# Batch 0's first pass in an attention and MoE kernel: casts shared out differently, the last sums on the matrix engine, weights loaded once

## The chip, the core and the metric

The kernel runs on one core of one Trainium2 chip. The metric is the device time of one execution in microseconds (us). A core has five engines that run side by side, each taking its own instructions in order: TensorE (PE: matmuls, PEld for its weight loads), VectorE (DVE), ScalarE (ACT), GpSimd (POOL) and SyncE (SP, which here only starts transfers). Transfers between the chip's memory and the core's SBUF are done by 16 DMA engines; a transfer is started by an instruction on POOL or SP.

## The reference

```python
def _attn_ref(x, inducing):          # x: 4 x 12480 x 128, inducing: 32 x 128
    scale = 1.0 / np.sqrt(C)
    I = np.broadcast_to(inducing[None], (B, m, C))
    def mab(q, kv):
        s = scale * (q @ kv.transpose(0, 2, 1))
        s = s - s.max(-1, keepdims=True)
        a = np.exp(s)
        a /= a.sum(-1, keepdims=True) + 1e-09
        return a @ kv
    h = mab(I, x)                    # 32 rows of each batch from all its rows
    return mab(x, h)

def _moe_ref(x, w_in, w_out):        # w_in: 128 x 2048, w_out: 2048 x 128
    h = x @ w_in
    relu6 = np.clip(h + 3.0, 0.0, 6.0)
    g = h * relu6 / 6.0
    return g @ w_out
```

The output is the second function applied to the rows of the first, 49920 x 128 in float32.

## The kernel before, in words

Each of the four batches goes through three phases.

**Phase A** reads the batch's 12480 rows once, in seven groups (`groups`, numbered 0 to 6): six of 128 partitions x 16 rows (1 MB each) and one of 96 x 2 rows. For each group the rows are cast to bf16 (`a_cast`, in quarters 0 to 4 of the 16 rows), transposed on PE into PSUM and copied out by DVE (`a_T`, two halves, L290 and L291), multiplied by the inducing rows (`a_s1`, L298), exponentiated on ACT (L304), and summed with those weights on PE (`a_agg`, L314, into the PSUM tile `hnd`). The denominators are summed by DVE over all groups in `dacc` (L325, L327).

**Phase C** reduces `dacc` (`c_sum`, L419), forms the 32 denominators on PE and divides (`c_den`, L432 to L438), transposes the result H (`c_HT`), and derives from it a small matrix product with the MoE weights: sixteen blocks `c_sq` (matmul L583, squared on ACT L594 or DVE L591 and L592) and `c_C` (L603), and `c_G3` (L489), `c_hs`, `c_L`, `c_BD` (L573, L577) for a linear part. `w_low` (L916, POOL) makes the low halves of w_in that `c_G3` reads.

**Phase B** passes over the batch's rows again, in 25 chunks, mainly on PE (L827, L856, L875) with ACT, DVE and POOL beside it, and writes the output. It needs `Cq` (`c_tail`) and `BD`.

Batch 0's phases A and C stand alone at the start (`a_first`, `c_first`); the order of every instruction on every engine there is written out by hand. From then on the kernel's main loop runs phase B of a batch, with the phases A and C of the next batch spliced in by position (`a_units`, `c_units`, `bg`). The order on each engine is the order of the program, so an instruction that waits holds up all that follow it on its engine.

`warm(n)` issues n matmuls of 512 columns with no use for their result. The rows of x come in five buffers (`XBUF`): the load of group 5 waits for group 0's buffer. Loads start on POOL's queue, in program order with POOL's casts. In `a_first` the cast of group g+1 is issued ahead of the transposes of group g:

```python
for g in range(NGR):
    if g + 1 < NGR:
        cast(g + 1)          # 3/4 on ACT, 1/4 on POOL (groups 1 to 3) or DVE
    a_T(0, g, 0)
    ...
    a_T(0, g, 1)
    ...
    if late:
        a_agg(0, g - 1, 0, late)
        a_agg(0, g - 1, 1, late)
    a_s1(0, g)
```

`load_weights` brings w_in and w_out twice each: once cast to bf16 by the transfer (`w_in_b`, `w_out_b`), once in float32 (`w_in_r`, two halves, and `w_out_r`).

Of the kernel before, what the change touches and what calls it, by code (L numbers as in the profile page):

```python
# [24 lines left out]
TG = 16  # L25
# [5 lines left out]
CASTLEAD = 1.6  # L31

# [18 lines left out]
def kernel(  # L51
# [40 lines left out]
    with ExitStack() as es:  # L92
# [71 lines left out]
        def load_weights(i):  # L164
            w_out = moe_w_out.rearrange("(kb kp) c -> kp kb c", kp=P)
            if i == 0:
                nc.gpsimd.dma_start(w_in_b[:, :], moe_w_in[:, :])
            elif i == 1:
                nc.gpsimd.dma_start(w_out_b[:, :, :], w_out)
                for h in range(2):  # L170
                    t = dgp.tile([P, F // 2], FP32R, name="w_in_r", tag="dg")
                    nc.gpsimd.dma_start(t[:, :], moe_w_in[:, h * F // 2 : (h + 1) * F // 2])
                    w_in_r.append(t)
                nc.gpsimd.dma_start(w_out_r[:, :, :], w_out)
# [25 lines left out]
        eng.memset(ones[:, :], 1.0)  # L200
        blk_f = const.tile([P, P], FP32, name="blk_f")
# [17 lines left out]
        for i in range(2):  # L219
            t = const.tile([P, 512], FP32R, name=f"BD{i}")  # L220
            eng.memset(t[:, :].bitcast(FP32), 0.0)
            BD.append(t)
# [70 lines left out]
        def a_s1(b, g):  # L293
            t0, p, n = groups[g]
            st = S[b]
            s1 = side_bank(b, [P, 512], FP32, "s1")
            for i in range(n):
                nc.tensor.matmul(  # L298
                    s1[:p, i * M : (i + 1) * M],
                    lhsT=st[("xT", g)][:, i * p : (i + 1) * p],  # L300
                    rhs=I_T[:, :],
                )
            a1 = a1p.tile([P, TG * M], FP32R, name="a1")
            nc.scalar.activation(a1[:p, : n * M], s1[:p, : n * M], ACT.Exp, scale=scale)  # L304
            st["a1"] = a1

        def a_agg(b, g, h, a1):
            t0, p, n = groups[g]
            st = S[b]
            lo, hi = (0, n // 2) if h == 0 else (n // 2, n)  # L310
            if g == 0 and h == 0:
                st["hnd"] = psH.tile([P, 512], FP32, name="hnd", tag="hnd")
            for i in range(lo, hi):
                nc.tensor.matmul(  # L314
                    st["hnd"][:M, :C],
                    lhsT=a1[:p, i * M : (i + 1) * M],
                    rhs=xs[(b, g)][:p, i, :],
                    start=(g == 0 and i == 0),
                    stop=(g == NGR - 1 and i == n - 1),
                )  # L320
            if h == 0:
                if b == 0 and g == NGR - 1:
                    pass
                elif g == 0:
                    nc.vector.tensor_copy(st["dacc"][:p, : n * M], a1[:p, : n * M].bitcast(FP32))  # L325
                else:
                    nc.vector.tensor_add(  # L327
                        st["dacc"][:p, : n * M], st["dacc"][:p, : n * M], a1[:p, : n * M].bitcast(FP32)
                    )
            else:  # L330
                if b == 0 and g == NGR - XBUF:
                    load_weights(1)
                load_next(b, g)
                if b == 0 and g == NGR - XBUF - 1:
                    load_weights(0)
# [48 lines left out]
        def a_first():  # L384

            def cast(g):
                eng = nc.gpsimd if 1 <= g <= 3 else nc.vector
                a_cast(0, g, ((nc.scalar.copy, 0, 2), (nc.scalar.copy, 2, 3), (eng.tensor_copy, 3, 4)))

            a_cast(0, 0, ((nc.scalar.copy, 0, 2), (nc.scalar.copy, 2, 4)))  # L390
            late = None
            for g in range(NGR):
                if g + 1 < NGR:
                    cast(g + 1)
# [4 lines left out]
                if g == 0:  # L399
                    warm(4)  # L400
                if late:
                    a_agg(0, g - 1, 0, late)
                    a_agg(0, g - 1, 1, late)
                a_s1(0, g)
                if g == 0:
                    warm(4)
                late = S[0]["a1"]
            half_rows()
            a_agg(0, NGR - 1, 0, late)
            a_agg(0, NGR - 1, 1, late)  # L410


        def c_sum(b, main=True):

            st = S[b]
            dred = cst.tile([P, M], FP32, name="dred" if main else "dred1")
            src = st["dacc"] if main else st["a1"].bitcast(FP32)
            p, n = (P, TG) if main else groups[-1][1:]
            nc.vector.tensor_reduce(  # L419
                dred[:p, :],  # L420
                src[:p, : n * M].rearrange("p (s m) -> p m s", m=M),
# [3 lines left out]
            st["dred"] = st.get("dred", []) + [dred[:p, :]]  # L425

        def c_den(b):
            st = S[b]
            dps = psF.tile([P, 512], FP32, name="dps", tag="fb")
            dred = st.pop("dred")  # L430
            for k, d in enumerate(dred):
                nc.tensor.matmul(  # L432
                    dps[:M, :2], lhsT=d, rhs=ones[: d.shape[0], :], start=(k == 0), stop=(k == len(dred) - 1)
                )
# [116 lines left out]
        def c_L(b, h):  # L551
# [15 lines left out]
            nc.vector.tensor_scalar_mul(L[:, :], lp[:M, :C], -1.0 / 6.0)  # L567
            st["L"] = L

        def c_BD(b):  # L570
# [4 lines left out]
            for q in range(4):  # L575
                eng = nc.vector.tensor_copy if q % 2 else nc.scalar.copy
                eng(bd[32 * q : 32 * q + 32, q * C : (q + 1) * C], lt[32 * q : 32 * q + 32, :C])  # L577
# [79 lines left out]
        def c_first():  # L657

            c_sum(0)
            c_sum(0, False)  # L660
            warm(2)
# [13 lines left out]
            for i in range(F // 256):  # L675
                w_low(i)
            bg(-3.5)
            load_held(3, len(held))
            for jb in range(3, 6):
                sq(jb)  # L680
                cs(jb - 3)
            b_f(0, 0)
            b_base(0, 0, 0)
            b_base(0, 0, 1)
            sq(6)
            cs(3)
# [226 lines left out]
        def w_low(i):  # L913
            lo, hi = i * 256, (i + 1) * 256
            t, at = w_in_r[2 * lo // F], lo % (F // 2)
            nc.gpsimd.tensor_sub(w_in_l[:, lo:hi], t[:, at : at + 256].bitcast(FP32), w_in_b[:, lo:hi])  # L916
# [257 lines left out]
```

## Time and profile before

| | us |
|---|---|
| median of 3 runs (310.03 to 311.34) | 310.95 |
| the profiled execution's own time | 310.18 |
| its span, first to last instruction | 308.3 |
| outside the span | 1.88 |
| group 1, 2, 3, 4, 5 of x at hand (ACT's cast starts) | 9.64, 12.19, 14.68, 18.44, 21.10 |
| transposes of groups 3, 4, 5 start on PE | 15.78, 20.33, 23.89 |
| the division of batch 0 (L436) starts | 29.78 |
| main loop's first matmul (L856) | 47.17 |
| last matmul of the main loop ends, about | 302.5 |

All times after the fourth line are counted from the span's start, in the profiled execution. PE is busy 94% of the span, DVE 76%, ACT 73%, POOL 38%. In the lines of the timeline that the prediction shows, the columns are: start, duration, engine, line of the kernel, operation, what it writes <- what it reads with the shapes, the number of instructions merged, and in square brackets the engine's idle time ahead of them with what ended it. The end of a PE row includes the time until the result can be read; the spacing of rows, not their duration, is what an engine needs for one.

### The profile page before, as it was taken

How to read it: one execution, taken by the hardware profiler on the slowest of the kernel's cores; microseconds unless marked ns; L12 is line 12 of the kernel's file. 1: busy time of each engine (PE TensorE's matmuls, PEld its weight loads, DVE VectorE, ACT ScalarE, POOL GpSimd, SP SyncE). 2: the span in 40 equal slices, each digit the busy share in tenths (PEclk: the TensorE clock that was granted, in tenths of full speed). 3: DMA queues.
4: the chain of work that ended last, by engine and by line, in shares of the span. 5: the costliest groups of instructions: out<-in, count | busy, mean ns of one | idle time of the engine just before them, and what ended most of it. 6: DMA issues, size and time to landing. Idle time of an engine off the chain costs nothing. (4 is left out here: it accounts for less than half of the span.)

```text
span 308.3 us, 9788 instructions
## 1 busy us (share of the span) xinstructions
PE 288.8 (94%) x3942; PEld 230.3 (75%) x3963; DVE 234.3 (76%) x499; ACT 224.9 (73%) x431; POOL 117.4 (38%) x234
## 2 busy tenths in 40 slices
PE   8978989999999899999998999998898999999992
PEld 3876577989888678777887977786687777777881
DVE  1567757887998578678897859788877885988893
ACT  3662769776968989668798899665696787777760
POOL 8460852431019995010097745000577760000000
PEclk9989999999999999999999999999999999999997
DMA  6999779699965547979628425256445565576753
GB/s 218 423 288 323 199 253 373 210 378 307 361 204 163 194 151 228 393 225 291 223 57 308 164 64 179 95 159 198 157 135 139 179 197 184 177 235 216 214 205 120
DMA packets 27441, 67.73 MB, mean 220 GB/s; under 512 B 5216, under 2 KB 20352, under 8 KB 21504
## 3 DMA queue, kind: packets, MB, share of 16 engines
q1 hardware_dynamic: 18784, 38.36, 38.4%
q0 software_dynamic: 8608, 28.71, 31.0%
q8 instruction: 32, 0.52, 0.7%
q14 instruction: 17, 0.14, 0.1%
HBM read 29.77 MB, written 25.56 MB: 179 GB/s over the span
## 5 line engine op out<-in xcount | busy, mean ns | idle before, releaser
L834 ACT ACTIVATE TF<-bp 128x512 bf16<-128x512 f32 (+1 forms) x200 | 115.6, 589 | 33.4 <-PE bp L827 17.9
L875 PE MATMUL op<-Cq,TF 128*128 128x128 bf16 (+1 forms) x784 | 104.7, 221 | 0.3
L875 PE MATMUL op<-Cq,TD 128*128 128x128 bf16 (+1 forms) x784 | 102.5, 219 | 0.0
L892 DVE TENSOR_TENSOR os<-op,r_all 128x512 f32<-128x512 f32 (+1 forms) x100 | 67.4, 674 | 23.5 <-PE op L875 18.9
L845 DVE TENSOR_TENSOR TD<-TF,d 128x1024 bf16<-128x1024 bf16 (+1 forms) x100 | 75.6, 756 | 4.3 <-ACT TF L834 3.3
L875 PEld LDWEIGHTS <-TF 128*128 128x128 bf16 (+1 forms) x784 | 55.1, 98 | 24.1 <-issue 12.7
L827 PE MATMUL bp<-xT,W 128*128 128x512 bf16 (+1 forms) x184 | 68.6, 375 | 2.2 <-DVE nf_all L753 1.0
L875 PEld LDWEIGHTS <-TD 128*128 128x128 bf16 (+1 forms) x784 | 60.3, 98 | 0.7 <-issue 0.2
L856 PE MATMUL op<-BD,nf 128*128 128x512 f32 (+1 forms) x100 | 52.3, 523 | 0.2 <-DVE os L892 0.2
L279 ACT CAST xb<-xr 128x512 bf16<-128x512 f32 (+1 forms) x70 | 45.3, 661 | 8.2 <-DMA xr<-in_x_dram 8.1
L291 DVE COPY xT<-pt 128x1024 bf16<-128x1024 bf16 (+1 forms) x56 | 34.0, 616 | 16.7 <-PE pt L290 15.8
L519 POOL TENSOR_TENSOR dg<-G 128x256 f32<-128x256 f32 x48 | 40.1, 836 | 0.0
L518 POOL TENSOR_TENSOR dg<-G 128x256 f32<-128x256 f32 x48 | 31.3, 653 | 14.6 <-ACT sq L526 10.1
L516 POOL COPY gate<-TD 128x1 bf16<-128x1 bf16 x48 | 11.7, 244 | 62.3 <-DVE TD L845 61.6
L526 ACT ACTIVATE sq<-dg 128x512 bf16<-128x512 f32 x48 | 30.3, 633 | 2.9 <-POOL dg L519 2.9
L314 PE MATMUL hnd<-xr,a 128*32 128x128 f32 x384 | 31.8, 229 | 0.6 <-ACT a L304 0.6
L290 PE MATMUL pt<-ident_b,xb 128*128 128x128 bf16 x392 | 30.9, 222 | 0.0
L603 PE MATMUL cp<-w_out_b,sq 128*128 128x128 bf16 x256 | 24.7, 219 | 2.5 <-ACT TF L834 1.3
L314 PEld LDWEIGHTS hnd<-xr,a 128*32 128x32 f32 x384 | 25.5, 111 | 1.7 <-ACT a L304 0.7
L783 PE MATMUL rp<-one,nf 128*128 128x4 f32 (+1 forms) x100 | 26.2, 264 | 0.5 <-ACT TF L834 0.5
L290 PEld LDWEIGHTS <-xb 128*128 128x128 bf16 x392 | 24.1, 99 | 2.8 <-issue 1.3
L806 ACT ACTIVATE dk<-pp 128x512 bf16<-128x512 f32 (+1 forms) x28 | 15.6, 556 | 12.3 <-PE pp L799 11.3
(127 smaller groups left out, 384.5 us busy)
## 6 DMA issues: line engine op xcount, KB each, us to landing
xr<-in_x_dram POOLq DMA_DIRECT2D x23, 1024.0 KB, 7.7
out_dram<-os SPq DMA_DIRECT2D x23, 1024.0 KB, 4.1
d<-dk SPq DMA_DIRECT2D x96, 128.0 KB, 4.4
xr<-in_x_dram POOLq DMA_DIRECT2D x2, 512.0 KB, 4.7
w_in_r<-in_moe_w_in_dram POOLq DMA_DIRECT2D x2, 512.0 KB, 10.7
w_out_r<-in_moe_w_out_dram POOLq DMA_DIRECT2D x1, 1024.0 KB, 14.1
out_dram<-os SPq DMA_DIRECT2D x4, 256.0 KB, 3.5
w_in_b<-in_moe_w_in_dram POOLq DMA_DIRECT2D x1, 512.0 KB, 7.7
```

What stands on the lines that cost most here:

```text
L279: eng(xb[:p, lo:hi, :], xs[(b, g)][:p, lo:hi, :].bitcast(FP32))
L290: nc.tensor.transpose(pt[:, (i - lo) * p : (i - lo + 1) * p], xb[:p, i, :], ident_b[:p, :p])
L291: nc.vector.tensor_copy(st[("xT", g)][:, lo * p : hi * p], pt[:, : (hi - lo) * p])
L314: nc.tensor.matmul(st["hnd"][:M, :C], lhsT=a1[:p, i * M : (i + 1) * M], rhs=xs[(b, g)][:p, i, :], start=(g == 0 and i == 0), stop=(g == NG ...
L518: nc.gpsimd.tensor_sub(dg[:, 0], stepped(G2, jb, 0, 1, 0), stepped(G2, jb, 2, 0, 2))
L519: nc.gpsimd.tensor_sub(dg[:, 1], stepped(G2, jb, 1, -1, 0), stepped(G2, jb, 10, 0, 2))
L827: nc.tensor.matmul(bp[:, :w], lhsT=st["W"][:, k].rearrange("p m i -> p (m i)"), rhs=st[("xT", g)][:, j * w : (j + 1) * w],)
L834: nc.scalar.activation(st[("x", c)][:, k, :w], bp[:, :w], ACT.Exp, scale=scale)
L845: nc.vector.tensor_mul(u[:, :, :w], t[:, :, :w], d[:, :w].unsqueeze(1).to_broadcast([P, 2, w]))
L856: nc.tensor.matmul(op[:p, : S_ * C], lhsT=st[("nf", g)][:R, j * p : (j + 1) * p], rhs=st["BD"][:R, : S_ * C], start=True, stop=False, skip ...
L875: nc.tensor.matmul(op[:p, s * C : (s + 1) * C], lhsT=T[k][:, s * p : (s + 1) * p], rhs=st["Cq"][:, k, :], start=False, stop=(s == S_ - 1 a ...
L892: nc.vector.tensor_mul(ot[:p, j * S_ : (j + 1) * S_, :], op[:p, : S_ * C].rearrange("p (s c) -> p s c", c=C), r_all[:p, b, c, :S_].unsquee ...
```

## The change

In `a_first`, the cast of group g is now issued in its own iteration: half on ACT, a quarter on DVE and a quarter on POOL (groups 1 to 3), or half on DVE (groups 4 and 5); group 6 is cast by POOL. The exponentials of a group follow the next group's cast on ACT. Two `warm` matmuls follow the scores of groups 0 to 4. `half_rows` moves to iteration 2. The scores and exponentials of group 5 are done in two halves, and the PE sums of group 5 come after the scores of group 6. The denominators of groups 4 to 6 are summed on PE (`a_den`, matmuls of 32 x 2 into `dps`) in place of DVE's additions; `c_sum` reduces the first four groups only, ahead of the last sums. The weights are loaded once, in float32, in pieces; the bf16 copy of w_in is made by two ACT casts (`w_in_cast`), that of w_out by four POOL casts (`w_out_cast`), and the eight `w_low` are split four and four around the end of phase A. `c_BD` is one DVE multiplication by a mask in place of four copies, and BD is no longer zeroed at the start. `c_first` has a new order.

```diff
 
-        def load_weights(i):
+        def load_w_in():
+            for h in range(2):
+                t = dgp.tile([P, F // 2], FP32R, name="w_in_r", tag="dg")
+                nc.gpsimd.dma_start(t[:, :], moe_w_in[:, h * F // 2 : (h + 1) * F // 2])
+                w_in_r.append(t)
+
+        def load_w_out(lo, hi):
             w_out = moe_w_out.rearrange("(kb kp) c -> kp kb c", kp=P)
-            if i == 0:
-                nc.gpsimd.dma_start(w_in_b[:, :], moe_w_in[:, :])
-            elif i == 1:
-                nc.gpsimd.dma_start(w_out_b[:, :, :], w_out)
-                for h in range(2):
-                    t = dgp.tile([P, F // 2], FP32R, name="w_in_r", tag="dg")
-                    nc.gpsimd.dma_start(t[:, :], moe_w_in[:, h * F // 2 : (h + 1) * F // 2])
-                    w_in_r.append(t)
-                nc.gpsimd.dma_start(w_out_r[:, :, :], w_out)
+            for j in range(4 * lo, 4 * hi, 4):
+                nc.gpsimd.dma_start(w_out_r[:, j : j + 4, :], w_out[:, j : j + 4, :])
+
+        def w_in_cast(eng, h):
+            eng(w_in_b[:, h * F // 2 : (h + 1) * F // 2], w_in_r[h][:, :].bitcast(FP32))
+
+        def w_low(i):
+            lo, hi = i * 256, (i + 1) * 256
+            t, at = w_in_r[2 * lo // F], lo % (F // 2)
+            nc.gpsimd.tensor_sub(w_in_l[:, lo:hi], t[:, at : at + 256].bitcast(FP32), w_in_b[:, lo:hi])
+
+        def w_out_cast(lo, hi):
+            for j in range(4 * lo, 4 * hi, 4):
+                nc.gpsimd.tensor_copy(w_out_b[:, j : j + 4, :], w_out_r[:, j : j + 4, :].bitcast(FP32))
...
         eng.memset(ones[:, :], 1.0)
+        one_r = const.tile([P, 2], FP32R, name="one_r")
+        eng.tensor_copy(one_r[:, :], ones[:, :])
...
-            t = const.tile([P, 512], FP32R, name=f"BD{i}")
-            eng.memset(t[:, :].bitcast(FP32), 0.0)
-            BD.append(t)
+            BD.append(const.tile([P, 512], FP32R, name=f"BD{i}"))
...
+        def a_den(g, h, a1):
+
+            t0, p, n = groups[g]
+            st = S[0]
+            lo, hi = (0, n // 2) if h == 0 else (n // 2, n)
+            if "dps" not in st:
+                st["dps"] = psF.tile([P, 512], FP32, name="dps", tag="fb")
+                first = True
+            else:
+                first = False
+            for i in range(lo, hi):
+                nc.tensor.matmul(
+                    st["dps"][:M, :2],
+                    lhsT=a1[:p, i * M : (i + 1) * M],
+                    rhs=one_r[:p, :],
+                    start=first and i == lo,
+                    stop=False,
+                    skip_group_check=True,
+                )
...
             if h == 0:
-                if b == 0 and g == NGR - 1:
-                    pass
+                if b == 0 and g >= SUMG:
+                    a_den(g, 0, a1)
                 elif g == 0:
                     nc.vector.tensor_copy(st["dacc"][:p, : n * M], a1[:p, : n * M].bitcast(FP32))
                 else:
...
                         st["dacc"][:p, : n * M], st["dacc"][:p, : n * M], a1[:p, : n * M].bitcast(FP32)
                     )
             else:
+                if b == 0 and g >= SUMG:
+                    a_den(g, 1, a1)
                 if b == 0 and g == NGR - XBUF:
-                    load_weights(1)
-                load_next(b, g)
-                if b == 0 and g == NGR - XBUF - 1:
-                    load_weights(0)
+                    load_w_in()
+                elif b == 0 and g == NGR - XBUF + 1:
+                    load_w_out(0, 2)
+                    load_next(0, NGR - XBUF)
+                    load_next(0, g)
+                elif b == 0 and g == NGR - XBUF + 2:
+                    load_w_out(2, 4)
+                    load_next(0, g)
+                else:
+                    load_next(b, g)
...
         def a_first():
-            def cast(g):
-                eng = nc.gpsimd if 1 <= g <= 3 else nc.vector
-                a_cast(0, g, ((nc.scalar.copy, 0, 2), (nc.scalar.copy, 2, 3), (eng.tensor_copy, 3, 4)))
-            a_cast(0, 0, ((nc.scalar.copy, 0, 2), (nc.scalar.copy, 2, 4)))
-            late = None
-            for g in range(NGR):
-                if g + 1 < NGR:
-                    cast(g + 1)
+            act, dve, pool = nc.scalar.copy, nc.vector.tensor_copy, nc.gpsimd.tensor_copy
+            last = NGR - 1
+            a1s, sc = {}, {}
+            def scores(g):
+                sc[g] = a_scores(0, g, 0, groups[g][2])
+            def weigh(g):
+                a1s[g] = a1p.tile([P, TG * M], FP32R, name="a1")
+                a_exp(0, g, sc.pop(g), 0, groups[g][2], a1s[g])
+            for g in range(last):
+                if g:
+                    a_cast(0, g, ((act, 2, 4), (dve, 0, 1), (pool if g < last - 2 else dve, 1, 2)))
+                    weigh(g - 1)
+                else:
+                    a_cast(0, g, ((act, 0, 2), (act, 2, 4)))
                 a_T(0, g, 0)
                 if g == 0:
                     warm(5)
                 a_T(0, g, 1)
-                if g == 0:
+                if g:
+                    a_agg(0, g - 1, 0, a1s[g - 1])
+                    a_agg(0, g - 1, 1, a1s[g - 1])
+                else:
                     warm(4)
-                if late:
-                    a_agg(0, g - 1, 0, late)
-                    a_agg(0, g - 1, 1, late)
-                a_s1(0, g)
-                if g == 0:
-                    warm(4)
-                late = S[0]["a1"]
-            half_rows()
-            a_agg(0, NGR - 1, 0, late)
-            a_agg(0, NGR - 1, 1, late)
-        def c_sum(b, main=True):
-            st = S[b]
-            dred = cst.tile([P, M], FP32, name="dred" if main else "dred1")
-            src = st["dacc"] if main else st["a1"].bitcast(FP32)
-            p, n = (P, TG) if main else groups[-1][1:]
+                if g == 2:
+                    half_rows()
+                if g < last - 1:
+                    scores(g)
+                    warm(2)
+            w_in_cast(act, 0)
+            a_cast(0, last, ((pool, 0, 4),))
+            a_T(0, last, 0)
+            a_T(0, last, 1)
+            n = groups[last - 1][2]
+            a1 = a1p.tile([P, TG * M], FP32R, name="a1")
+            for lo, hi in ((0, n // 2), (n // 2, n)):
+                a_exp(0, last - 1, a_scores(0, last - 1, lo, hi), lo, hi, a1)
+            scores(last)
+            weigh(last)
+            c_sum(0)
+            w_in_cast(act, 1)
+            for i in range(4):
+                w_low(i)
+            w_out_cast(0, 1)
+            a_agg(0, last - 1, 0, a1)
+            a_agg(0, last - 1, 1, a1)
+            a_agg(0, last, 0, a1s[last])
+            a_agg(0, last, 1, a1s[last])
+        def c_sum(b):
+            st = S[b]
+            dred = cst.tile([P, M], FP32, name="dred")
             nc.vector.tensor_reduce(
-                dred[:p, :],
-                src[:p, : n * M].rearrange("p (s m) -> p m s", m=M),
+                dred[:, :],
+                st["dacc"][:, : TG * M].rearrange("p (s m) -> p m s", m=M),
                 axis=AX.X,
                 op=ALU.add,
             )
-            st["dred"] = st.get("dred", []) + [dred[:p, :]]
+            st["dred"] = dred
...
-            dps = psF.tile([P, 512], FP32, name="dps", tag="fb")
-            dred = st.pop("dred")
-            for k, d in enumerate(dred):
-                nc.tensor.matmul(
-                    dps[:M, :2], lhsT=d, rhs=ones[: d.shape[0], :], start=(k == 0), stop=(k == len(dred) - 1)
-                )
+            dps = st["dps"] if b == 0 else psF.tile([P, 512], FP32, name="dps", tag="fb")
+            nc.tensor.matmul(
+                dps[:M, :2], lhsT=st["dred"][:, :], rhs=ones[:, :], start=(b > 0), stop=True, skip_group_check=True
+            )
...
-            nc.vector.tensor_scalar_mul(L[:, :], lp[:M, :C], -1.0 / 6.0)
+            nc.vector.tensor_scalar_mul(L[:, :], lp[:M, :C], 1.0 / 6.0)
...
-            for q in range(4):
-                eng = nc.vector.tensor_copy if q % 2 else nc.scalar.copy
-                eng(bd[32 * q : 32 * q + 32, q * C : (q + 1) * C], lt[32 * q : 32 * q + 32, :C])
+            nc.vector.tensor_mul(
+                bd[:, :].rearrange("p (q c) -> p q c", c=C),
+                lt[:, :C].unsqueeze(1).to_broadcast([P, 4, C]),
+                one4_f[:, :].unsqueeze(2).to_broadcast([P, 4, C]),
+            )
...
-            c_sum(0)
-            c_sum(0, False)
-            warm(2)
...
             nc.gpsimd.tensor_copy(made[:, :], S[0]["W"][:, 0, 0, 0:1])
-            for i in range(F // 256):
+            w_out_cast(1, 2)
+            for i in range(4, F // 256):
                 w_low(i)
+            w_out_cast(2, 3)
             bg(-3.5)
+            w_out_cast(3, 4)
             load_held(3, len(held))
-            for jb in range(3, 6):
-                sq(jb)
-                cs(jb - 3)
             b_f(0, 0)
+            sq(3)
+            cs(0)
+            sq(4)
+            cs(1)
             b_base(0, 0, 0)
             b_base(0, 0, 1)
+            sq(5)
+            cs(2)
             sq(6)
             cs(3)
+            c_G3(0, 0, 16)
+            c_hs(0)
             sq(7)
             cs(4)
             sq(8)
             cs(5)
+            bg(-3.0)
             sq(9)
-            c_G3(0, 0, 8)
             cs(6)
-            c_G3(0, 8, 16)
-            c_hs(0)
+            c_L(0, 0)
+            c_L(0, 1)
             sq(10)
             cs(7)
-            bg(-3.0)
             b_prod(0, 0)
-            sq(11)
-            cs(8)
-            c_L(0, 0)
-            c_L(0, 1)
-            sq(12)
-            cs(9)
-            bg(-2.0)
-            b_base(0, 1, 0)
-            sq(13)
-            cs(10)
             b_r(0, 0)
             b_r(0, 1)
             c_BD(0)
+            sq(11)
+            cs(8)
+            bg(-2.0)
+            b_base(0, 1, 0)
+            sq(12)
+            cs(9)
+            b_base(0, 1, 1)
+            sq(13)
+            cs(10)
+            bg(-1.0)
             sq(14)
             cs(11)
-            bg(-1.0)
             sq(15)
             cs(12)
-            b_base(0, 1, 1)
             cs(13, 14, 15)
```

More of the change, by code (lines that the diff above doesn't have):

```diff
@@ L31 @@
 CASTLEAD = 1.6
+SUMG = 4
 def shifted(t, off, k_step, i_step):
@@ L294, in a_s1, with a_scores, a_exp @@
             t0, p, n = groups[g]
-            st = S[b]
+            S[b]["a1"] = a1p.tile([P, TG * M], FP32R, name="a1")
+            a_exp(b, g, a_scores(b, g, 0, n), 0, n, S[b]["a1"])
+        def a_scores(b, g, lo, hi):
+            t0, p, n = groups[g]
             s1 = side_bank(b, [P, 512], FP32, "s1")
-            for i in range(n):
+            for i in range(lo, hi):
                 nc.tensor.matmul(
                     s1[:p, i * M : (i + 1) * M],
-                    lhsT=st[("xT", g)][:, i * p : (i + 1) * p],
+                    lhsT=S[b][("xT", g)][:, i * p : (i + 1) * p],
                     rhs=I_T[:, :],
                 )
-            a1 = a1p.tile([P, TG * M], FP32R, name="a1")
-            nc.scalar.activation(a1[:p, : n * M], s1[:p, : n * M], ACT.Exp, scale=scale)
-            st["a1"] = a1
+            return s1
+        def a_exp(b, g, s1, lo, hi, a1):
+            p = groups[g][1]
+            nc.scalar.activation(a1[:p, lo * M : hi * M], s1[:p, lo * M : hi * M], ACT.Exp, scale=scale)
+        def a_den(g, h, a1):
+            t0, p, n = groups[g]
+            st = S[0]
[5 more added lines that the diff above has]
+                first = False
+            for i in range(lo, hi):
+                nc.tensor.matmul(
[6 more added lines that the diff above has]
+                )
         def a_agg(b, g, h, a1):
@@ L911 @@
         plan = []
[L913 to L916, printed above, removed]
         for b in range(1, B):
```

## The prediction, on record before the changed kernel ran

> **What bounds the kernel now.** I read the page's slices first, then the waits, the timeline of the first 50 us, and the granted clock there in steps of 0.4 us.
>
> ```profile
> PE   8978989999999899999998999998898999999992
> PEclk9989999999999999999999999999999999999997
> ```
>
> From 50 us on PE has no gap of note that an earlier start would widen: the main loop is PE's. Of the edit, only `c_BD` and a matmul flag lie in it. So the change is worth what it moves the loop's first matmul (L856, at 47.17), and that is phase A to the division (29.78) and phase C from there (17.39). The third slice (15.4 to 23.1) has the low clock.
>
> ```profile
> DVE xT L291 <- PE pt L290: 8.5, 5, 3.9
> ACT xb L279 <- DMA xr<-in_x_dram: 8.1, 6, 3.6
> ...
> DVE xb L279 <- DMA xr<-in_x_dram: 3.0, 2, 2.5
> ```
>
> Casts wait for rows of x, DVE's too, though DVE has other work:
>
> ```profile
> 15.78 1.14 PE L290 MATMUL pt<-ident_b,xb 128*128 128x128 bf16 x16
> ...
> 18.43 0.43 DVE L279 CAST xb<-xr 128x512 bf16<-128x512 f32 x1 [2.55 <-DMA xr<-in_x_dram]
> ...
> 18.78 1.28 DVE L291 COPY xT<-pt 128x1024 bf16<-128x1024 bf16 x2
> 19.52 0.27 PEld L298 LDWEIGHTS <-xT 128*128 128x128 bf16 x8 [1.75 <-DVE xT L291]
> ...
> 20.33 1.56 PE L290 MATMUL pt<-ident_b,xb 128*128 128x128 bf16 x16
> ...
> 23.89 1.15 PE L290 MATMUL pt<-ident_b,xb 128*128 128x128 bf16 x16
> ...
> 28.31 1.03 DVE L419 TENSOR_REDUCE dred<-dacc 128x32 f32<-128x512 f32 x1
> ...
> 29.78 0.16 DVE L436 RECIPROCAL rD<-dps 32x1 f32<-32x1 f32 x1 [0.32 <-PE dps L432]
> ```
>
> Group 3's transposes were done at 16.9, but their copy stands behind group 4's cast on DVE, which waits for x until 18.43. PE stops from 17.95 to 19.52, and pays later:
>
> ```profile
> 18.60:19.00 0.40, 0.00 (x0) 1.00 1.01 312
> ...
> 20.60:21.00 0.40, 0.40 (x9) 0.62 1.25 251
> 21.00:21.40 0.40, 0.40 (x7) 0.50 0.97 195
> ...
> 23.80:24.20 0.40, 0.40 (x14) 0.61 1.97 222
> 24.20:24.60 0.40, 0.40 (x11) 1.00 1.66 217
> ```
>
> (Columns: PE busy, instructions, clock, DMA share, GB/s; from 18.60 to 19.00 PE did nothing.) From about 20.7 to 24.1 the clock is half.
>
> **Part by part: groups 1 to 5.** Before, a group takes what x takes: 2.5 us (casts at 9.64, 12.19, 14.68). Now DVE's order within a group is cast, two copies, the addition for the group before. Spacings from the rows: a quarter's cast 0.43, two in a row 0.77 (21.09 to 21.43, plus 0.43); hand-over 0.05; transposes to their first copy 0.65 (13.29 to 13.95); two copies 1.21 (13.95 to 15.16); an addition 0.60 (27.07 to 27.68). One group is 0.43 + 0.05 + 0.65 + 1.21 + 0.60 = 2.94, one with two DVE casts 3.28. Both are longer than x's 2.5, so DVE paces phase A and x runs ahead. PE's own sum for a group, 0.88 + 0.98 + 0.42 + 0.43 (transposes, sums, scores, `warm(2)`) = 2.71, hides under it.
>
> The chain: group 1 at 9.64; POOL's quarter (0.61) and `warm(2)` give transposes at 10.35, sums end 12.35. POOL starts the load of group 5 0.3 later (as at 13.01 to 13.30), 0.55, and only then casts group 2's quarter: this queue position is new. Transposes 2 at 13.9; copies from 14.55; addition 15.76; `half_rows` 16.36 (0.63, 27.68 to 28.31); cast 17.0; transposes 3 at 17.45 (before 15.78); 4 at 17.45 + 0.65 + 1.21 + 0.60 + 0.82 = 20.73 (20.33); 5 at 24.0 (23.89). x is at hand at 18.43 and 21.09: no wait. So the repaired stall is paid back by a longer round.
>
> **The tail.** From 24.0: transposes 0.88; group 4's sums 16 x 0.061 = 0.98 (1.15 less 0.17 of result delay); its new denominators, 16 matmuls with 2 columns. No row shows these. Nearest: 32-column ones at 0.025 (16 in 0.56), the sums themselves, same weights, at 0.061; L432 with the same two columns in full float32, 0.045. I take 0.03, near the short ones, as only the moving side shrinks: 0.48. Then group 6's transposes 0.11, scores of 5 0.42: 26.87. A half's result is there at about 26.85, its exponential 0.37, so sums from 27.25: 0.98 + 0.48, group 6 0.18, last matmul 0.30: the division at **29.2**, against 29.78. Gain 0.55. All 34 denominators at 0.025 make it 0.7, at 0.061 they turn it into a loss of 0.5. Taken off the path: `c_sum` (1.03 plus 0.21; now beside group 5's sums), two additions (0.60 each).
>
> The other edits here cost nothing while covered. Weights: half as many bytes behind x. `w_in_cast` needs the first half by 25.8, when ACT would else hold group 5's exponentials; w_in_b, in that place before, landed at 15.80 + 7.7 = 23.5. Each us beyond 25.8 costs one. The second cast (1.04) ends at about 28.7, ahead of the HTb copy at about 30.4. POOL's four `w_low` (0.66 each) and one `w_out_cast` (0.61 for 512) end by 28.5 if the weights are there; the next POOL work waits for W at 31.6. Zeroing BD (0.97) was in POOL's idle time.
>
> **One rule against it.** POOL and DVE now both cast float32 when group 1 arrives. Before, DVE's product at 54.21 took 1.67 against 0.68 while POOL cast beside it: one stood behind the other. Here that is 0.43 + 0.61 in a row in place of 0.61; 0.3 later for group 1, passed on through POOL's queue to the end: gain 0.2 to 0.3 instead of 0.55. I take 0.45. [...]
>
> **Phase C, 17.39 now.** The order changes, the work on ACT and PE barely: of the path to the last square, ACT's BD copies leave (0.25 + 0.26, and 0.35 of wait), one TF (0.60) comes ahead of the last squares. The new BD product (128x512 from PSUM, as L291's 0.69) is needed only by L856; before, BD was ready at 44.93 and L856 ran at 47.17, so its shorter chain is hidden. `c_G3` comes some 1.3 earlier, at about 35.3; POOL after W: 0.2 + 0.61 + 4 x 0.66 = 3.4, so its last `w_low` ends at 35.1, and PE reads it at 36.4. If that slack went, each 0.1 costs 0.1. The later `w_out_cast` stands behind the casts of batch 1's first group and ends at about 38.6; its reader came at 44.7 before. `load_held` starts at about 38.7 (39.73 before): earlier, hidden. ACT waits 0.84, 0.35 and 1.33 in 38 to 42 for PE; the earlier `c_L` can fill up to 1.3 of that. Against: matmuls L (1.15) now sit ahead of sq 10, and the TF. I take 0.15 gain, bounds 1.3 gain and 0.6 loss. In later batches `c_BD` trades two ACT copies for 0.1 more of DVE, within noise.
>
> **Sum.** 0.45 + 0.15 = 0.6: the profiled execution, 310.18 (308.3 and 1.88 around it), would be 309.6. It lies 0.77 under the median, so against 310.95 I say **310.3**. A measurement of this kernel can tell about 0.5%, 1.55 us, from none: this forecast is within it.
>
> **Rivals.**
> 1. *x paces, as before the change* (0.13). If DVE's round were under 2.5 us, transposes 5 would start at 21.09 + 0.82 = 21.9, 2.1 earlier than in my chain: 308.2. For: DVE was busy only 1.3 of each 2 us at 12 to 16. Against: the round's sum of spacings.
> 2. *Phase C closes up* (0.16). ACT's waits are filled: 0.45 + 1.3 = 1.75, 309.2. For: 2.5 us of waits behind `c_G3` and `c_L`. Against: the squares still alternate with PE one by one.
> 3. *Slower: weights ahead of the last exponentials* (0.08). Place: `w_in_cast` on ACT, in front of group 5's exponentials. It decides from a landing after 25.8. At the w_in_r rows' landing (17.49 + 10.7 = 28.2) it costs 2.4: 312.7. Against: those rows had both bf16 loads ahead of them.
> 4. *Half clock again* (0.08). 3.4 us at half rate lose 1.7 of PE's work; if on the tail, and with denominators at 0.061, 310.3 + 1.7 + 1.0 = 313.0. Before, 1.8 us idle out of 3.4 (17.3 to 20.7) preceded it; the window 24.1 to 27.5 with 0.7 idle did not bring it, and in my chain no 3.4 us have over 1.1. [...]
> 5. *It doesn't do what it says* (0.03): the casts gain nothing and x comes later; within 0.5%.
>
> **Numbers.** Forecast 0.52: within 0.5%. Faster: rivals 1 and 2, 0.29. Slower: 3 and 4, 0.16. Same: 0.52 + 0.03 = 0.55. The likeliest case alone spans 309.2 to 312.0 (denominators at 0.061, 1.05 more, and phase C 0.75 more). The range reaches to rival 2, and near 1, below, and short of 3 above: 308.3 to 312.3.
>
> **What would show it.** Right: transposes 3, 4, 5 at about 17.5, 20.7, 24.0 with DVE never waiting for x from group 3 on; clock 1.00 through 30 us; L436 at about 29.3; the 34 `a_den` matmuls within 1.0 us together; L856's counterpart about 0.6 ahead of 47.17. Wrong: transposes 5 near 22, an ACT wait for w_in_r, a clock of 0.50 before 30 us, or PE waiting for `w_low`.

## The result

| | before | after |
|---|---|---|
| median, same chip, us | 310.95 (309.59 to 311.34, 5 runs) | 312.59 (311.49 to 313.02, 5 runs) |
| profiled execution, us | 310.18 | 311.49 |
| its span, us | 308.3 | 309.7 |
| division of batch 0, start | 29.78 | 29.05 |
| main loop's first matmul (L856; L927 after) | 47.17 | 47.01 |
| last chunk's first matmul, against before | 0 | +1.32 |

The ratio is 1.0064, interval [1.0039, 1.009]: slower by 1.64 us, just over the 1.55 us that can be told from none. The forecast was 310.3. The two profiled executions lie 1.31 apart. A half-clock window is a stretch of 3.41 us in which TensorE's granted clock is 0.50 (in before from 20.70 to 24.11). Executions of one kernel differ here mostly by the number of such windows in them (of the five of after, two had a mean clock of 0.994 and took 311.49 and 311.89, three 0.989 or 0.990 and took 312.59 to 313.02; one window takes 0.0055 off the mean over 310 us), each worth 0.7 to 1.4 us in the profiles. Apart from the last microseconds, the profiled execution of after has none, and that of before has the one in phase A.

**Phase A** came as forecast. The page's slices show the clock of after without the dip in the third slice:

```profile
PE   8889979999999899979998999988899999999992
...
PEclk9999999999999999999999999999999999999997
```

Timeline of after, 16 to 30 us (start, duration, engine, line, operation; in brackets the idle time ahead):

```profile
17.61 1.07 PE L302 MATMUL pt<-ident_b,xb 128*128 128x128 bf16 x16 [0.93 <-DVE xb L291]
...
20.55 1.18 PE L302 MATMUL pt<-ident_b,xb 128*128 128x128 bf16 x16 [0.28 <-DVE xb L291]
...
23.64 1.18 PE L302 MATMUL pt<-ident_b,xb 128*128 128x128 bf16 x16 [0.31 <-DVE xb L291]
...
25.13 0.39 PE L336 MATMUL dps<-one_r,a 128*32 128x2 f32 x8
...
29.05 0.15 DVE L503 RECIPROCAL rD<-dps 32x1 f32<-32x1 f32 x1 [1.36 <-PE dps L499]
```

Transposes of groups 3, 4 and 5 were forecast for 17.45, 20.73 and 24.0, the division for 29.3. Eight denominators last 0.39, and each of them 0.17 by its own record; their starts lie 0.03 apart, so that is what one adds.

**Phase C** took most of the 0.73 back. In the timeline of after, PE stands for 1.04 us at `c_BD`'s matmul, since L (L634) waits its turn on DVE behind a square and a copy; ACT then has no square to make until 41.67:

```profile
39.18 0.69 DVE L661 TENSOR_TENSOR sq<-d,dpm 128x512 bf16<-128x512 f32 x1 [0.53 <-DVE d L660]
...
39.79 0.68 DVE L303 COPY xT<-pt 128x1024 bf16<-128x1024 bf16 x1
40.39 0.27 DVE L634 TENSOR_SCALAR L<-lp 32x128 f32<-32x128 f32 x1
...
40.80 0.45 PE L640 MATMUL lt<-L,sel 32*128 32x128 f32 x2 [1.04 <-DVE L L634]
...
41.67 0.60 ACT L663 ACTIVATE sq<-dpm 128x512 bf16<-128x512 f32 x1 [1.68 <-PE dpm L652]
```

From division to loop: 17.39 before, 17.96 after.

**The main loop** is where the 1.3 us come from, and the prediction had nothing there. I lined up the start of every chunk's first matmul (L856 and L927; chunks 0 to 99, 25 to a batch) in the two timelines: after leads by 0.16 at chunk 0; that grows by 1.01 at chunk 22, by 0.41 at 45 and 46, by 0.24 at 70; it loses 1.55 at chunk 27, and 1.59 at 52. Sum: -0.16 - 1.66 + 3.14 = +1.32.

The gains are `c_BD` of batches 1 to 3, each made while the batch before it is in the loop. Timeline of before, around the first of them:

```profile
112.70 0.25 ACT L577 CAST BD<-lt 32x128 fp32r<-32x128 f32 x1 [0.20 <-PE lt L573]
112.98 0.28 DVE L577 CAST BD<-lt 32x128 fp32r<-32x128 f32 x1 [0.41 <-ACT BD L577]
113.30 0.26 ACT L577 CAST BD<-lt 32x128 fp32r<-32x128 f32 x1 [0.35 <-DVE BD L577]
...
113.59 0.30 DVE L577 CAST BD<-lt 32x128 fp32r<-32x128 f32 x1 [0.32 <-ACT BD L577]
```

The four copies go one after the other, each engine waiting for the other's, and both engines' next work stands behind. In after one product stands in their place:

```profile
112.53 0.69 DVE L642 TENSOR_TENSOR BD<-lt,one_f 128x512 fp32r<-128x512 f32 x1
```

The losses are waits for the output store. The output tile `os` has two buffers; where a batch ends, the small group 6 takes the second one right after group 5, so the next batch's group 0 needs group 5's buffer before the store of 1 MB out of it has landed. In the waits of after (total, times, longest):

```profile
DVE os L963 <- DMA out_dram<-os: 3.8, 1, 3.8
...
DVE os L963 <- PE ep L806: 2.3, 1, 2.3
DVE os L963 <- PE pp L870: 1.8, 1, 1.8
```

and in those of before:

```profile
DVE BD L577 <- ACT BD L577: 3.5, 7, 1.3
...
DVE os L892 <- PE rp L783: 2.2, 1, 2.2
DVE os L892 <- PE pp L799: 1.8, 1, 1.8
```

The releasers `rp`, `pp` and `ep` had long been done; each of these rows is the same store wait. Before waits at the ends of batches 0 and 2, after at those of batches 0, 1 and 2, and longer at the first. The store at the end of batch 1 is issued at about the same time in both (198.35 and 198.32), but in after it lands later. Of each kernel's transfers between 198 and 208 us, before and then after (KB, us from issue to landing):

```profile
out_dram<-os SPq DMA_DIRECT2D x1, 1024.0 KB, 4.0
```

```profile
out_dram<-os SPq DMA_DIRECT2D x1, 1024.0 KB, 5.7
```

In the trace's packets (128 of 8 KB for this store), 97% had ended at 201.86 (before) and 201.90 (after), but the last one ended at 202.00 and at 203.52. Each of the two traces also has 32 packets of 16 KB in a queue of the kind `instruction`, fetches of instructions: one for 247 (before) and 249 (after) records of TensorE's matmuls and weight loads, 7905 and 7973 in all, where no other engine has over 499. In after such a fetch runs from 201.63 to 202.51, in the tail of the store; in before the fetch of the same number, the 22nd, starts at 203.45, behind the store. The packets also show what stands behind the fetch: one packet of the store starts at 202.50, when the fetch ends, and takes 0.72, where the median packet of the store takes 0.32; one more runs behind it, to 203.52.

The change itself moved the fetch. Counted in the traces by what they write, after has 34 matmuls of `a_den` and 4 more of `warm`, and 2 fewer of `c_den`: 36 more, with their weight loads 72 more TensorE instructions, all ahead of the loop.

### The profile page after: what moved, and what is told of

It is laid out like the page before. It is cut to its first block, busy times and chain, and to the rows that moved or that the text cites. A ratio compares the mean times of both kernels' runs of the same rounds, so it can differ in the third digit from the quotient of the medians.

```text
span 309.7 us, 9847 instructions
## 1 busy us (share of the span) xinstructions
PE 287.3 (93%) x3974; PEld 229.8 (74%) x3999; DVE 234.8 (76%) x496; ACT 222.4 (72%) x420; POOL 120.4 (39%) x239
## 5 line engine op out<-in xcount | busy, mean ns | idle before, releaser
L927 PE MATMUL op<-BD,nf 128*128 128x512 f32 (+1 forms) x100 | 52.3, 523 | 1.8 <-DVE os L963 1.8
L291 ACT CAST xb<-xr 128x512 bf16<-128x512 f32 (+1 forms) x65 | 42.8, 665 | 9.7 <-DMA xr<-in_x_dram 9.7
L586 POOL TENSOR_TENSOR dg<-G 128x256 f32<-128x256 f32 x48 | 40.6, 846 | 0.0
L585 POOL TENSOR_TENSOR dg<-G 128x256 f32<-128x256 f32 x48 | 31.8, 662 | 13.5 <-ACT sq L593 8.8
L133 POOL DMA_DIRECT2D xr<-in_x_dram x25 | 13.8, 554 | 33.2 <-PE rp L854 11.4
L352 PEld LDWEIGHTS hnd<-xr,a 128*32 128x32 f32 x384 | 24.8, 109 | 1.1 <-issue 0.7
```

The lines of the kernel that those rows point to most:

```text
L291: eng(xb[:p, lo:hi, :], xs[(b, g)][:p, lo:hi, :].bitcast(FP32))
L352: nc.tensor.matmul(st["hnd"][:M, :C], lhsT=a1[:p, i * M : (i + 1) * M], rhs=xs[(b, g)][:p, i, :], start=(g == 0 and i == 0), stop=(g == NG ...
L585: nc.gpsimd.tensor_sub(dg[:, 0], stepped(G2, jb, 0, 1, 0), stepped(G2, jb, 2, 0, 2))
L586: nc.gpsimd.tensor_sub(dg[:, 1], stepped(G2, jb, 1, -1, 0), stepped(G2, jb, 10, 0, 2))
L927: nc.tensor.matmul(op[:p, : S_ * C], lhsT=st[("nf", g)][:R, j * p : (j + 1) * p], rhs=st["BD"][:R, : S_ * C], start=True, stop=False, skip ...
```

## The experiments

Theory: a fetch of TensorE instructions that falls into a store's tail holds its last packets up, `os` waits, and so does the loop. Rivals: the waits belong to the new order of the work; or the whole loss is phase C's.

**The kernels of the first comparison.** The changed kernel again, and `c_BD` of batch 0 two steps later:

> The changed kernel once more, for a second profile and five more runs. In its first profile the loop's first matmul (L927) ran at 47.01 (47.17 before), and VectorE's write of the output tile (L963) then stood 3.76 us at 132.29 and 2.26 us at 204.17 behind a store. Theory 'store wait' (the loop's loss is that a store of one group's output lands too late for its buffer to be used again): waits of 1 us and more at the same two places, where a batch ends, in every profile, and a median near 312.4. Rival 'chance': the waits are elsewhere or absent, and the median falls to 311 or less. Theory 'half clock' (some runs have one more 3.4 us at half clock): runs with a mean clock near 0.989 are 1.2 to 1.5 us longer than those near 0.994; if this profile is one of the former, its place is seen.

> The changed kernel with c_BD(0) issued after block 9 of c_C in place of after block 7. Theory 'BD wait' (phase C lost 0.6 us because TensorE stands 1.04 us at c_BD's matmul for VectorE's scaling of L, with ScalarE idle 1.68 us behind it): no wait at that matmul, and the loop's first matmul 0.8 to 1.2 us after 45.0, that is at 45.8 to 46.2, against 47.01. Rival 'pace of the squares' (phase C is set by the alternation of squares and products, and the wait only shows slack): the loop's first matmul within 0.3 us of 47.0. The total need not follow, as the loop's waits on stores can take it back: 311 to 312.6 by the first theory.

```diff
             b_r(0, 1)
-            c_BD(0)
             sq(11)
...
             cs(9)
+            c_BD(0)
```

The output tile in halves, four buffers of half the size, each stored when full; for both kernels:

> The kernel before with the same halved output tile. Theory 'store wait': it gains less than the changed kernel does, 1 to 2.5 us (its own waits were 2.21 at 131.92 and 1.83 at 261.84): 308.5 to 310, and it and the changed kernel with halves are then within 0.5 us of each other. Rival 'elsewhere': it keeps its lead of 1.6 us over the changed kernel with halves.

> The changed kernel with the output tile in halves (four buffers of 8 rows in place of two of 16, each stored when it is full; same memory, all output computed). Theory 'store wait': no wait of VectorE on a store above 0.3 us, and 1.5 to 3.5 us less than the changed kernel: 309 to 311. Rival 'elsewhere' (the loop loses by something else, such as half clock or queues on GpSimd): within 0.5 us of the changed kernel's 312.6.

```diff
-        osp = es.enter_context(tc.tile_pool(name="osp", bufs=2))
+        osp = es.enter_context(tc.tile_pool(name="osp", bufs=4))
...
-            if j == 0:
-                st["os"] = osp.tile([P, TG, C], FP32, name="os")
+            if j % 2 == 0:
+                st["os"] = osp.tile([P, TG // 2, C], FP32, name="os")
```

Beside before at 311.02: the changed kernel again 313.07, ratio 1.0059 [1.003, 1.0088], with its store waits at the same places and two half-clock windows in its profiled execution (314.91); `c_BD` late 312.96, 1.0069 [1.0034, 1.0104]; halves: before 308.88, 0.9927 [0.9899, 0.9955], after 306.86, 0.9868 [0.9839, 0.9897].

With halves no `os` waits for a store, and the same change that lost 1.6 us gains 2.0. The theory had put the two halved kernels within 0.5 of each other: it did not have the gain of `c_BD` in the loop. Part of the 2.0 is probably the window in phase A: three of the seven executions of before with halves took 307.9 to 308.1 (the profiled one, which has no window, is one of them), four 308.9 to 309.2. The two profiled executions lie 1.11 apart.

With `c_BD` late the loop starts at 46.34 instead of 47.01, against 45.8 to 46.2 expected: PE's stop at `c_BD` is what phase C lost. But the store waits took that back, and more than expected (311 to 312.6): of a lead, a wait for a store leaves nothing when the store does not land earlier with it.

**Moving the fetches.** Two kernels that change nothing but the number of TensorE instructions in the warm-up:

> The kernel before with 36 more matrix multiplies (72 more TensorE instructions with their weight loads) in its warm-up: the 8 multiplies of 512 columns before the first transposes are 44 of 64 columns. Nothing else differs. Theory (the 16 KB fetches of TensorE instructions decide when the output stores land): every fetch of the loop comes about 2.6 us earlier, the one at 203.5 near 201, inside the store of group 5 of batch 2 (first packet about 198, last 202.0 before); the output write at chunk 52 then waits 1 to 2 us for its buffer, and the kernel takes 311.5 to 313. Rival (the wait at chunk 52 comes from the changed order of the work, not from the fetches): loop start and waits as before, 310.3 to 311.3, no wait at chunk 52.

```diff
-        warm(8)
+        warm(44, 64)
```

(the second number: columns of each).

> The changed kernel with 92 more matrix multiplies (184 more TensorE instructions) in its warm-up, in smaller pieces of about the same total time, so that each instruction fetch comes 256 - 184 = 72 instructions (about 2.6 us) later in the loop than in the changed kernel: 129.6 to about 132, 201.8 to about 204.4, both behind the last packets of the two stores. Theory: the waits at chunks 27 and 52 shrink by 1 to 2 us each and the kernel takes 309.3 to 311, level with the kernel before or below. Rival (fetches do not matter): 312.5 to 313.2, waits as in the changed kernel.

```diff
-        warm(4)
+        warm(28, 64)
...
-        warm(8)
+        warm(60, 48)
...
-                    warm(5)
+                    warm(13, 160)
...
-                    warm(4)
+                    warm(12, 128)
```

Beside before at 310.66: before with 72 more took 314.05, 1.011 [1.0061, 1.0159], beyond the 313 of the theory; after with 184 more 310.77, 1.0025 [0.9992, 1.0058]. The first is 3.4 us slower for a few empty multiplies at the start, though its loop starts 0.93 earlier than before's. The 72 are as many as the change adds. The store at the end of batch 1 in it, and in after with 184 more:

```profile
out_dram<-os SPq DMA_DIRECT2D x1, 1024.0 KB, 5.8
```

```profile
out_dram<-os SPq DMA_DIRECT2D x1, 1024.0 KB, 4.0
```

In the first, the fetch runs from 204.37 to 205.25, 97% of the store's packets have ended at 204.30, and the last one starts at 205.24 and ends at 205.95; in the second no fetch falls between first and last packet (198.62 to 201.40). (The expectation's "batch 2" is this batch, 1 when counted from 0.) The wait at chunk 52 came (+1.62) and went (from +1.59 to -0.01) with it. At this place the rival falls: the order of the work was not touched.

At chunk 27 it does not fall. In the second kernel +1.01 is left there of +1.55, and that is not the fetch, which now runs from 131.01 to 131.94: no packet of the store starts at its end. The last three packets run one after another from 130.37 to 131.29, after two of the store that took 1.12 and 1.24. The store was issued 1.17 earlier than in before (123.97 against 125.14) and landed only 0.16 earlier (131.29 against 131.45), so the lead that `c_BD` had won at chunk 22 was lost. Why the store took so much longer stays open. Of the 1.55, then, 0.5 is the fetch and 1.0 the lead.

Two more things came out otherwise. At the end of batch 1 the fetches moved by about 1.5 us of the loop's work and not 2.6 (the expectation has 256 instructions for a fetch, the pages 247 and 249 records). And at chunk 27 the first kernel waited longer than expected, with the fetch (129.50 to 130.38) in the store's tail and seven packets of the store one after another behind it, to 132.92; DVE timeline:

```profile
133.55 0.69 DVE L892 TENSOR_TENSOR os<-op,r_all 128x512 f32<-128x512 f32 x1 [4.79 <-DMA out_dram<-os]
```

PE's pause there was 2.79 us, and from 134 to 138 the clock was 0.57 in the mean. The pauses of the second execution of after (2.34) and of `c_BD` late (2.13) had such a window behind them too; those of 1.76 (after) and 1.22 (after with 184 more) had none. So a late packet cost its wait, and where the pause was over 2 us another 0.8 to 1.4. The profiled execution of after with 184 more has one window of its own near 225, behind two pauses of 1.28 and 0.48 that after has too (+1.36).

**Which edit gains.** With halves the executions of the changed kernel agree within 0.23 us, and parts of the change can be told apart.

> The changed kernel with the output tile in halves (306.86 in the last comparison), and c_BD of batches 1 to 3 as four copies on ACT and DVE again instead of one product on DVE; batch 0 keeps the product. Theory (the one product takes ACT out of the chain in the loop and is worth the 1.0, 0.35 and 0.23 us seen at chunks 22, 45 and 70): 308.3 to 308.6, the loss at those chunks. Rival (these gains were the work coming out otherwise, as the prediction had it: within noise): 306.7 to 307.1.

> The kernel before with the output tile in halves (308.88 in its comparison), and c_BD of batches 1 to 3 as one product on DVE; batch 0 keeps the four copies. Theory (of the change, the loop gains only by this product): 1.6 to 1.8 less, 307.1 to 307.4, at chunks 22, 45 and 70. Rival (the product's gain needs the rest of the change): 308.5 to 309.

```diff
-            for q in range(4):
-                eng = nc.vector.tensor_copy if q % 2 else nc.scalar.copy
-                eng(bd[32 * q : 32 * q + 32, q * C : (q + 1) * C], lt[32 * q : 32 * q + 32, :C])
+            if b == 0:
+                ...
+            else:
+                nc.vector.tensor_mul(
+                ...
```

(the second kernel; the first has the branches the other way round). After with four copies again: 308.67, 0.9934 [0.9908, 0.9961], 1.8 more than with the product, just above the expected range. Before with the product: 306.50, 0.9847 [0.9822, 0.9872], 2.4 less than without, more than the 1.6 to 1.8 expected; the lowest times of the two (306.03 and 307.88) lie 1.85 apart, and a half-clock window more or less is in the rest. The steps are the same wherever it is: in before with halves, -1.01, -0.40 and -0.24 at chunks 22, 45 and 70. That one edit in the loop is nearly all that the change has gained: before with halves and the product took 306.03 at its best, and the fastest version here 305.66 at its best.

> The changed kernel with the output tile in halves and c_BD of batch 0 two steps later (behind sq 12 and C 9). With c_BD late alone the loop's first matmul came 0.67 us earlier and the waits for stores took it back. Theory (only those waits took it back): loop start near 46.3, 306.0 to 306.4. Rival (the loop gives the earlier start back in other waits): 306.7 to 307.1.

306.03, 0.9845 [0.9802, 0.9887], as expected: with the store waits gone, the loop starts 0.88 earlier than in after with halves (46.24 against 47.12), and 0.83 of that reaches the end. The same edit with whole tiles had brought nothing.

**Phase A.**

> The kernel before, unchanged, profiled once more, for its phase A alone. In the profiled execution that the prediction rests on, TensorE had a window at half clock from 20.0 to 24.3 and the division began at 29.78; with the output tile in halves, and with the longer warm-up, the same phase A had no such window and divided at 29.09 and 28.86. Theory (the window is an accident of one execution, and phase A of before at full clock is as fast as the new one): no window near 20 us, division at 28.9 to 29.2. Rival (the window belongs to the kernel before and the new phase A takes it away): window again, division at 29.7 to 29.8.

One more execution of before: 310.64, division at 29.84 and the window again (clock 0.66 and 0.50 from 20 to 24). The theory as I put it falls: the window is no accident of one execution. Of five profiles with the old phase A, three had it (before, this one, before with the product: PE's pause 1.58, 1.66 and 1.74), two not (halves: pause 1.82; 72 more: 1.22 and 0.48). Of the eight with the new phase A none had it. Without it, the timeline of before with halves:

```profile
20.64 1.05 PE L290 MATMUL pt<-ident_b,xb 128*128 128x128 bf16 x16
23.32 1.05 PE L290 MATMUL pt<-ident_b,xb 128*128 128x128 bf16 x16
...
29.09 0.15 DVE L436 RECIPROCAL rD<-dps 32x1 f32<-32x1 f32 x1 [0.32 <-PE dps L432]
```

At full clock the old phase A is as fast as the new (division at 29.09 and 28.86, against 29.05 to 29.30 in the eight): the change gains 0.7 there in executions that would have had the window, and nothing in others. Since phase C is longer in after, its loop then starts later: 47.12 against 46.48 with halves.

> The changed kernel with the output tile in halves and c_BD of batch 0 late (306.03), with the sums of groups 4 and 5 of batch 0 back on DVE; only the small group 6 is summed on TensorE, and the reduction follows the addition of group 5. Theory (the sums on TensorE take the last addition out of DVE's chain; the one of group 4 fits in a pause of DVE of 0.7 us before 26.5): division at 29.5 to 29.7 instead of 29.21, 306.3 to 306.6. Rival (what DVE saves, TensorE's 34 small multiplies cost): division within 0.1, 306.0 to 306.1.

```diff
-SUMG = 4
+SUMG = 6
...
             weigh(last)
-            c_sum(0)
...
             a_agg(0, last - 1, 1, a1)
+            c_sum(0)
```

305.79, 0.9829 [0.9804, 0.9854]: below both ranges, though the rival had the division right, within 0.1. It is 0.10 *earlier* (29.11), and the loop starts 0.52 earlier (45.72). Around the division in the kernel with the sums on TensorE, and then with those of groups 4 and 5 on DVE:

```profile
29.21 0.15 DVE L503 RECIPROCAL rD<-dps 32x1 f32<-32x1 f32 x1 [1.35 <-PE dps L499]
```

```profile
28.85 0.22 PE L499 MATMUL dps<-ones,dred 128*32 128x2 f32 x2 [0.57 <-DVE dred L488]
```

With them on TensorE, DVE is idle for 1.35 us after its reduction and PE ends last; on DVE, PE waits 0.57 for the reduction. The two come out within 0.1, so the sums moved from one path to another of the same length. Of the 0.52, 0.4 appears only at 39.4, where a copy on DVE follows a square that here did not wait; why it waited 0.53 in the other kernel stays open. This is the fastest version of the study, 5.3 us under before in its comparison, and nearly all of that is the halved tile and `c_BD` (the product in the loop, the later place in batch 0).

## Why the prediction was wrong

- **"The change is worth what it moves the loop's first matmul"**, because "PE has no gap of note that an earlier start would widen". This step failed, and decided the sign. In the loop lay waits for stores, and at two of them after lost 1.55 and 1.59: 2.1 of that because the 72 instructions that the change adds ahead of the loop put a fetch into the tails of two stores, 1.0 because a lead was lost to a store that did not land with it. The waits of before had two rows of store waits, 2.2 and 1.8, under wrong releasers. I read the slices of PE, 7.7 us each, in which they hardly show, and I priced the 34 denominators by their time on PE alone.
- **"In later batches `c_BD` trades two ACT copies for 0.1 more of DVE, within noise"** failed too, the other way: 1.66 gained. The row that shows it, ACT and DVE waiting for each other's copies, 3.5 us, was there as well. I had counted the instructions and not what stands behind them.
- **Phase C, "0.15 gain, bounds 1.3 gain and 0.6 loss"**: 0.57 lost, at the lower bound. "Its shorter chain is hidden" looked at when BD is read and not at where its matmul stands in PE's order: it waited 1.04 for L there, and two steps later it cost nothing.
- **Phase A** was right in its rows: starts within 0.4, the clock, denominators at 0.03, w_in in time. The division gained 0.73, forecast 0.45. Its reason was not: the gain is the half-clock window, which the working had in its durations of before without a price of its own; that an execution of before without it would gain nothing here was not seen, so that 0.73 lies near 0.45 is luck. The prediction's DVE round of 2.94 is right for after (17.61 to 20.55), but the old round is 2.68 at full clock (20.64 to 23.32).
- **The rule against it** held for this cast: POOL's of group 1 took 0.87 in after (from 9.76) beside DVE's of 0.43 (from 9.73), and 0.61 alone in before; 0.26 of the 0.3 taken. It ended 0.47 after DVE's; one wholly behind the other would make that 0.61. Why POOL's is slower there, no row shows.
- **Rivals**: x did not pace, the weights were not late, and the half clock did not return in phase A. Phase C did not close up, it grew. None of the five was a wait in the loop, and so 0.16 for slower was too little.

What the runs leave open: why the packet behind a fetch takes 0.72 and not 0.3 (packets of the next transfer, `d`, are in the same queue at that time), and why the store at the end of batch 0, issued 1.17 earlier, took 1.0 longer to land with no fetch in its way.

## What to carry to other kernels

Before an early stage is costed by what it moves the main loop, read the main loop's own waits row by row, and ask of each whether what it waits for moves with the start; a row whose releaser was long done may be a transfer, as the rows of `os` were here. A buffer that is free only just in time turns any shift, even one of instructions fetched, into microseconds: give it slack first (here worth 2.1 us without the change, 6.2 with it), and then measure the rest of the change. A half-clock window in the profiled execution is priced by itself, since it may not be the kernel's.

## What the runs showed of the hardware

- Beside the kernel's transfers before and after each have 32 instruction fetches of 16 KB, of 0.88 to 1.61 us. With one in its tail a store of 1 MB landed after 5.7 us instead of 4.0 (end of batch 1; after, before), and with empty multiplies at the start of the program, 72 instructions, one ran there in before too, 200 us later (5.8). In eight stores at a batch's end (both profiles of after, `c_BD` late, before with 72 more), one packet of the store starts within 0.02 us of the end of a fetch in its tail and takes 0.71 or 0.72. In both profiles of before a fetch starts 0.05 to 0.07 ahead of such a store's last packet; there no packet starts at its end, and the store is not late. At chunk 52 the loop lost 1.59 in after and 1.62 in before with 72 more, where a fetch stood ahead of the store's last packets, and nothing (-0.01) in after with 184 more, where none did.
- The clock fell after PE pauses of 1.58 to 1.74 us in three profiles (before twice, before with halves and the product) and not after 1.82 and 1.76 in two others (before with halves, after), so a pause's length alone does not decide it. In the traces' record of the clock, the stretch from the rise at the start to the first fall is a whole number of times 3.41 us: 13.65 (4 times; falls near 20.7), 129.71 (38; falls between 134 and 136), 218.45 (64; after with 184 more). Cut each run into steps of 3.41 from that rise: in eight of the nine steps that end with a fall before the program's end, PE's idle time (no row of a matmul) was 1.74 to 2.79; in the ninth it was 1.51, and of all others none has more than 1.55. The pause of 1.82 lies across two steps (0.94 and 1.11 idle in them), those of 1.58 to 1.74 each within one (1.81 to 1.97).
